# Attention and two gated feed-forward layers: the issue order of all engines is chosen by a search over priorities

## The chip, the core and the metric

The kernel runs on one core of a Trainium2 chip. The core has five engines that run their own instruction queues in order: TensorE (PE, matrix products, with its weight loads shown apart as PEld), VectorE (DVE), ScalarE (ACT), GpSimd (POOL) and SyncE (SP, which issues the DMA transfers here). An instruction waits until the semaphores it names have been raised, and all that stands behind it on its engine waits with it. The metric is the device time of one execution in microseconds (us).

## The reference

Two batches of eight heads, 768 positions, head size 64. Each position attends to the 31 positions around it and to 24 block summaries (maximum of the keys, mean of the values, over blocks of 32). The result, 1536 tokens of 512, goes through two feed-forward layers.

```python
k_sum = k.reshape(B, H, nb, block, D).max(axis=3)
v_sum = v.reshape(B, H, nb, block, D).mean(axis=3)
scores_l = scale * np.matmul(q, k.transpose(0, 1, 3, 2))      # kept where |i - j| < 16
scores_s = scale * np.einsum('bhsd,bhnd->bhsn', q, k_sum) + np.log(block)
a = softmax(concatenate([scores_l, scores_s]))
x = a @ concatenate([v, v_sum])                # -> 1536 x 512
x = (silu(x @ w_gate) * (x @ w_val)) @ w_out   # d_ff 1536
h = x @ w_in2
out = (h * tanh(softplus(h))) @ w_out2         # d_ff 2048
```

## The kernel before

**Attention** is cut into 24 units: batch, third of the sequence, pair of heads (four pairs). A unit has a piece on TensorE for the scores (`scores`, S below, line 468), on VectorE four passes that add the mask and take the extreme (line 504), on ScalarE four exponentials (line 521), on VectorE the division (lines 534 to 544), on TensorE four transposes (`transposes`, T, line 558) whose result ScalarE copies out of PSUM, and on TensorE the products with the values (`values`, V, line 573). ScalarE and VectorE then cut the result into two fp32r halves `xh` and `xl`. Units 0 to 3 are those of the first 256 tokens.

**The means** of the values of batch 0 (`means_first`) are six products of line 346 (M below), one for each of six loads m0 to m5, added up in PSUM bank 0. Four copies then bring the result into `vext`, the value windows: pair 0 and 2 on ScalarE (line 279), 1 and 3 on VectorE (line 285). All four read bank 0. Every V of the first batch needs its pair's copy.

**Weights** come as 64-bit words of a float64 array in loads of 512 KB (`words32`, t0, t1, ... below, into three buffers `raw`); ScalarE (line 725) and VectorE (lines 732, 741, 752) make 32-bit floats of them, and the two engines cut these into fp32r halves in `wsl`. The first three are the gate, value and output weights of chunk 0.

**The feed-forward work** is a list of items (chunk of the hidden size, token group). The first items have 256 tokens. H below is a product of line 822 (hidden layer), O one of lines 873 and 921 (output layer). Later units of seven block products use line 1179. At the end of a run of items VectorE adds the output banks to `pacc` (line 952), and a new run may write the bank only after that.

**The order.** The kernel does not issue as it goes. `Program.add` records operations with an engine, a cost, the keys they read and write, and at times a wanted time. `Program.order` then goes through them with a list scheduler on a model: each engine takes the ready operation with the earliest latest time. What it gives is the order in which every engine's queue is written. The model sees handover times, DMA times and costs as constants; nothing of it exists on the chip. The loads of the beginning have wanted times from `FIRST_LOADS`: k, q are the keys and queries of a unit, c0 and c1 the two halves of the constants (masks; last mask, identity and mean matrix), m the mean loads, w the value windows of a unit, t the weights.

**Fills.** Where the model sees TensorE idle before line 873 begins, `order` puts products on a constant tile (`warm`, line 266, W below). They compute nothing that is used.

**Loads** share eight semaphores in turn, so that a load is issued only when the eighth before it has landed.

Of the kernel before, what the change touches and what calls it, by code (L numbers as in the profile page):

```python
# [56 lines left out]

JOIN, PAIRED = 6, 12


FIRST_LOADS = "k0 q0 k1 c0 q1 k2 c1 q2 k3 q3 t0 t1 m0 m1 m2 m3 m4 m5 w0 w1 w2 w3 t2".split()
# [36 lines left out]
class Program:  # L98
# [3 lines left out]
    def __init__(self):  # L102
        self.ops = []

        self.fill, self.fill_to = None, 0
        self.last_write = {}
        self.readers = {}

    def add(self, eng, cost, fn, r=(), w=(), want=None, rel=0.0):
# [15 lines left out]
        self.ops.append(dict(eng=eng, cost=cost, fn=fn, deps=sorted(deps), want=want, rel=rel))  # L125

    def order(self):
# [6 lines left out]
        dma_latency, hop = 3200.0, 250.0  # L134
        own = dict(PE=0.0, ACT=120.0, DVE=120.0, POOL=120.0, SP=0.0)
        late = [0.0] * len(ops)
        for n in range(len(ops) - 1, -1, -1):
            o = ops[n]
            t = min((late[s] for s in after[n]), default=1e9) - o["cost"] - hop
            if o["eng"] == "SP":  # L140
                t -= dma_latency
            late[n] = t if o["want"] is None else min(t, o["want"])
        left = [len(o["deps"]) for o in ops]
        ready = [o["rel"] for o in ops]
        free = dict.fromkeys(own, 0.0)
        dma_free = 1000.0
        waiting = {e: [n for n, o in enumerate(ops) if o["eng"] == e and not left[n]] for e in own}
        done = []
        while any(waiting.values()):
            best = None  # L150
            for e, c in waiting.items():
                if c:
                    t = max(free[e], min(ready[n] for n in c))
                    if e == "SP":
                        t = max(t, dma_free - 1500.0)
                    if best is None or t < best[0]:
                        best = (t, e)
# [4 lines left out]
            if e == "PE" and self.fill:  # L162
                gap = t - free["PE"]
                done += [self.fill] * (FILL_FIRST if not free["PE"] else max(0, int(FILL * gap / 430.0)))
                if n == self.fill_to:
                    self.fill = None
            done.append(o["fn"])
            if e == "SP":
                free[e] = t + 450.0
                dma_free = max(dma_free, t) + o["cost"]  # L170
                end = dma_free + dma_latency
            else:
                free[e] = end = t + o["cost"]
            for s in after[n]:
# [4 lines left out]
        return done  # L179
# [10 lines left out]
def c_pool(n):  # L190
    return 100 + 2.35 * n
# [7 lines left out]
def tile_kernel(  # L199
# [47 lines left out]
    vrows = vx[:, 0 : NPAIR * 512].rearrange("k (n c) -> k n c", c=DM)  # L247
    vext = [vrows[:, :, p * P : (p + 1) * P] for p in range(NPAIR)]
# [27 lines left out]
    def copy(dst, src, n, psum, r, w, scale=1.0, eng="ACT"):  # L276
# [3 lines left out]
        elif eng == "POOL":  # L280
            assert scale == 1.0
            cost, fn = c_pool(n) * 1.5, lambda: nc.gpsimd.tensor_copy(out=dst, in_=src)
# [85 lines left out]
    def means_second(side):  # L368
# [22 lines left out]
        op("PE", 920, products, r=[*used, "cst1"], w=[("bank", bk)])  # L391
# [84 lines left out]
    def scores(*of):  # L476
        vals = held.pop(of[0], [])
        made = [score_products(i) for i in of]
        cost = 530 * len(vals) + 410 * len(of) + 250 + 130 * (len(vals) > 0) + (300 if of[0] < NPAIR else 0)
# [13 lines left out]
    def softmax(i):  # L493
# [46 lines left out]
        op("DVE", 100, lambda: nc.vector.reciprocal(out=t[:, 2, :], in_=t[:, 2, :]), w=[kt_])  # L540
# [22 lines left out]
    def values(i):  # L563
# [29 lines left out]
        op("PE", 640, products, r=r, w=w, want=wanted_at(i) + 9e3)  # L593
# [27 lines left out]
    for step in steps:  # L621
        stage[step[0]](int(step[1:]))
# [84 lines left out]
    def words32(name, c):  # L707

        k = counts["raw"]
        counts["raw"] += 1  # L710
        rw, a, q = raw[k % NRAW], cva[k % NCV], cvs[k % NCV]
        kr, ka, kq = ("raw", k % NRAW), ("cva", k % NCV), ("cvs", k % NCV)
        src = w_src[name][c].bitcast(U32)
        if len(src.shape) == 3:
# [9 lines left out]
            650,  # L724
# [22 lines left out]
        if name in "gvo":  # L747
            return f32(a), ka
# [8 lines left out]
        )  # L757
        return f32(a), ka
# [484 lines left out]
    for n, it in enumerate(items):  # L1243
        if it[0] == 1 and it[4] == GRP:
            clock["rate"] = 1.0
        (block_item if it in blocked else silu_item)(n)
        while prev <= n - lag[n]:
            out_products(prev)
            prev += 1
        if n == first_s - AHEAD:  # L1250
# [61 lines left out]
```

## Time and profile before

| what | value |
|---|---|
| three timed runs | 605.57, 606.43, 609.68 us, median 606.43 us |
| the profiled execution's own time | 605.46 us |
| its span, first to last instruction | 603.5 us |
| TensorE busy | 594.7 us, 99% |
| VectorE, ScalarE, GpSimd busy | 443.8 us (74%), 332.3 us (55%), 25.0 us (4%) |
| granted TensorE clock, mean | 0.999 |

TensorE's busy time holds the fills and matmuls that are drawn out by waits in their pipeline, so it is to be read stage by stage and against the pace of the same products elsewhere. The chain that ended last is TensorE for 93% of the span.

### The profile page before, as it was taken

The page shows a single profiled execution, that of the slowest core. Times are in us where ns is not written, and L with a number is a line of the kernel's source. Part 1 is how long each engine was busy: PE and PEld are TensorE (multiplying, and loading weights), DVE is VectorE, ACT ScalarE, POOL GpSimd, SP SyncE. Part 2 cuts the span into 40 slices and gives each one's busy share as a digit, 9 for nine tenths or more (in the row PEclk, how much of TensorE's full clock was granted, in tenths as well). Part 3 has the DMA queues.
Part 4 walks back from the last instruction along what each step waited for, and adds up shares of the span by engine and source line. Part 5 has one row for each costly group of instructions (what it writes and reads, how often), then busy time and mean ns, then how long its engine had stood idle before and what let it go on. Part 6 is the DMA issues. An engine that isn't in the chain of part 4 may idle for free.

```text
span 603.5 us, 10209 instructions
## 1 busy us (share of the span) xinstructions
PE 594.7 (99%) x3858; PEld 507.2 (84%) x3858; DVE 443.8 (74%) x1005; ACT 332.3 (55%) x764; POOL 25.0 (4%) x37
## 2 busy tenths in 40 slices
PE   8999999999999999999999999999999999999997
PEld 6688899988988889988889778988888889988875
DVE  6898689687498958858948999996574476972333
ACT  4787689655464635634525666766553465643230
POOL 3213220000000000000000000000000000000000
PEclk9999999999999999999999999999999999999999
DMA  9988566004100321302401301332130040300103
GB/s 321 303 240 220 128 197 201 29 6 153 52 1 0 141 70 45 133 33 71 141 0 33 108 2 35 105 140 84 56 107 34 1 139 1 106 0 1 70 1 139
DMA packets 34768, 55.02 MB, mean 91 GB/s; under 512 B 8712, under 2 KB 23176, under 8 KB 34720
## 3 DMA queue, kind: packets, MB, share of 16 engines
q1 hardware_dynamic: 34720, 54.38, 28.4%
q8 instruction: 30, 0.49, 0.3%
q14 instruction: 18, 0.15, 0.1%
HBM read 50.98 MB, written 3.15 MB: 90 GB/s over the span
## 4 chain that ended last, share of the span: by engine, by line
PE 93%; DVE 3%; DMA 2%; ACT 1%; issue 0%; SPq 0%; DVEq 0%
PE bank L1179 38%; PE bank L921 34%; PE bank L822 11%; PE bank L873 3%; PE bank L468 2%; PE bank L573 2%; PE bank L558 2%; DMA raw<-in_w_gate_dram 1%; DVE pacc L952 1%; PE bank L346 1%; DMA att<-in_qt_dram 1%; DVE pacc L293 1%; PE bank L266 0%; DVE xl L1079 0%; PE bank L382 0%
## 5 line engine op out<-in xcount | busy, mean ns | idle before, releaser
L1179 PE MATMUL bank<-xh,wsl 128*128 128x256 f32 (+1 forms) x512 | 142.5, 336 | 0.0
L921 PE MATMUL bank<-wsl,gt 128*128 128x512 f32 x576 | 139.1, 390 | 0.2 <-DVE pacc L952 0.2
L921 PEld LDWEIGHTS bank<-wsl,gt 128*128 128x128 f32 x576 | 106.0, 188 | 20.8 <-ACT gt L279 0.6
L1179 PEld LDWEIGHTS bank<-xh,wsl 128*128 128x128 f32 x512 | 92.0, 189 | 11.2
L293 DVE TENSOR_TENSOR tmps<-tmps,bank 128x256 f32<-128x256 f32 (+1 forms) x93 | 51.3, 551 | 66.9 <-PE bank L1179 56.5
L921 PE MATMUL bank<-gt,wsl 128*128 128x512 f32 x360 | 92.3, 392 | 1.0 <-DVE pacc L952 0.6
L1179 PE MATMUL bank<-att_late,wsl 128*128 128x512 f32 (+1 forms) x352 | 86.8, 370 | 0.0
L1179 PE MATMUL bank<-xl,wsl 128*128 128x256 f32 (+1 forms) x256 | 85.9, 336 | 0.0
L279 ACT ACTIVATE wsl<-cva 128x512 fp32r<-128x512 f32 (+1 forms) x100 | 59.1, 594 | 41.7 <-DVE cva L752 10.1
L921 PEld LDWEIGHTS bank<-gt,wsl 128*128 128x128 f32 x360 | 65.7, 188 | 14.9 <-DVE pacc L952 2.0
L822 PE MATMUL bank<-xh,wsl 128*128 128x256 f32 (+1 forms) x288 | 77.9, 328 | 0.3 <-DVE tmps L1131 0.3
L1179 PEld LDWEIGHTS bank<-att_late,wsl 128*128 128x128 f32 x352 | 64.8, 188 | 12.1 <-ACT tmps L279 0.2
L293 DVE TENSOR_TENSOR wsl<-cva,wsl 128x512 fp32r<-128x512 f32 (+1 forms) x100 | 63.8, 644 | 11.4 <-ACT wsl L279 9.9
L279 ACT ACTIVATE tmps<-bank 128x512 f32<-128x512 f32 (+1 forms) x80 | 39.1, 491 | 56.4 <-PE bank L1179 49.8
L293 DVE TENSOR_TENSOR gt<-tmps,gt 128x512 fp32r<-128x512 f32 (+1 forms) x77 | 49.6, 644 | 25.7 <-PE bank L921 13.9
L279 ACT ACTIVATE gt<-tmps 128x512 fp32r<-128x512 f32 (+1 forms) x76 | 44.9, 591 | 29.7 <-PE bank L921 21.8
L1201 ACT ACTIVATE tmps<-tmps 128x512 f32<-128x512 f32 (+1 forms) x66 | 34.5, 522 | 48.3 <-DVE tmps L293 48.1
L822 PEld LDWEIGHTS bank<-xh,wsl 128*128 128x128 f32 x288 | 51.6, 189 | 6.8 <-issue 1.8
L1179 PEld LDWEIGHTS bank<-xl,wsl 128*128 128x128 f32 x256 | 48.4, 189 | 6.3
L741 DVE SCALAR_TENSOR_TENSOR cva<-cvs,cva 128x512 uint32<-128x512 uint32 x68 | 46.7, 691 | 1.2
L725 ACT ACTIVATE cvs<-raw 128x512 f32<-128x512 f32 x68 | 45.0, 667 | 3.5 <-DMA raw<-in_w_val_dram 1.7
L822 PE MATMUL bank<-xl,wsl 128*128 128x256 f32 (+1 forms) x144 | 45.8, 318 | 0.0
(104 smaller groups left out, 721.1 us busy)
## 6 DMA issues: line engine op xcount, KB each, us to landing
raw<-in_w_out_dram SPq DMA_DIRECT2D x28, 512.0 KB, 3.7
raw<-in_w_in_dram SPq DMA_DIRECT2D x16, 512.0 KB, 3.6
raw<-in_w_gate_dram SPq DMA_DIRECT2D x12, 512.0 KB, 3.5
raw<-in_w_val_dram SPq DMA_DIRECT2D x12, 512.0 KB
att<-in_vt_dram SPq DMA_DIRECT2D x24, 192.0 KB, 5.4
att<-in_qt_dram SPq DMA_DIRECT2D x24, 128.0 KB, 4.5
out_dram<-pacc SPq DMA_DIRECT2D x8, 256.0 KB, 2.1
pacc<-in_kt_dram SPq DMA_DIRECT2D x4, 400.0 KB, 5.0
```

The source lines that it names most:

```text
L279: cost, fn = c_act(n, psum), lambda: nc.scalar.activation(out=dst, in_=src, func=AF.Copy, scale=scale)
L293: op(eng, c_dve(n), lambda: nc.vector.tensor_tensor(out=dst, in0=a, in1=b, op=alu), r=r, w=w)
L468: nc.tensor.matmul(parts_[2 * j + n // 2][q, cols], qb[d, n, :], moving, start=True, stop=True)
L558: nc.tensor.transpose(ps[0:KC, n * P : (n + 1) * P], s[:, n * KC : (n + 1) * KC], ident)
L573: nc.tensor.matmul(ps[d, n * TQ : (n + 1) * TQ], ve[:, n, d], pt[:, at : at + TQ], start=True, stop=True)
L725: lambda: nc.scalar.activation(out=f32(q), in_=f32(high), scale=2.0**-112, **signed),
L741: lambda: nc.vector.scalar_tensor_tensor(out=a, in0=q, scalar=3, in1=a, op0=ALU.logical_shift_left, op1=ALU.bitwise_or),
L822: nc.tensor.matmul(ps, a, x, start=(kk == 0 and m == 0), stop=(kk == KD - 1 and m == 2))
L873: nc.tensor.matmul(bank[bk][:, col : col + HALF], w[:, a, mm], gg[:, x, 0:sz], start=(n in starts and both == 1 and q == 0 and m % 2 == 0) ...
L921: nc.tensor.matmul(bank[m], lhs, rhs, start=(n in starts and both == 1 and q == 0), stop=(n in ends and both == 0),)
L1179: nc.tensor.matmul(banks[b][:, 0:wide], w, v()[:, kk, :], start=(start and kk == 0 and m == 0), stop=(kk == 1 and m == 2), skip_group_chec ...
L1201: op("ACT", c_act(wide), lambda: nc.scalar.activation(out=y, in_=src, func=func), r=r, w=[*k, *free])
```

## The change

`order` now calls the list scheduler (moved into `issued`) 601 times: first as it is, then with shifts of the priorities of groups of operations, drawn with a fixed seed, of which each is kept if the model's last TensorE operation does not end later. Only groups with a latest time under 110 us are shifted. The model itself has other constants: handover 170 ns instead of 250, starting times for the engines, a DMA that lands 1650 ns after its bytes and at most eight loads in flight, VectorE and GpSimd not at once on what the model takes for a shared port, and other costs for some TensorE pieces, GpSimd copies and one ScalarE conversion. `FIRST_LOADS` has c0, c1 and the mean loads further ahead. The four value windows `vext` lie one behind the other in `att` instead of interleaved by 128 columns. The arithmetic is the same; the number of fills is what the new order makes it.

```diff
-FIRST_LOADS = "k0 q0 k1 c0 q1 k2 c1 q2 k3 q3 t0 t1 m0 m1 m2 m3 m4 m5 w0 w1 w2 w3 t2".split()
+RECIP = 100
+SEARCH, SEARCHED = 600, 110e3
+FIRST_LOADS = "k0 q0 c0 k1 q1 c1 m0 m1 k2 q2 k3 q3 m2 m3 t0 m4 m5 t1 w0 w1 w2 w3 t2".split()
...
+        groups = sorted({o["group"] for n, o in enumerate(ops) if o["group"] and late[n] < SEARCHED})
+        rng, shift = random.Random(0), dict.fromkeys(groups, 0.0)
+
+        def issue(shift):
+            return self.issued(after, [t + shift.get(o["group"], 0.0) for t, o in zip(late, ops)])
+
+        best, issued = issue(shift)
+        for _ in range(SEARCH):
+            other = dict(shift)
+            for g in rng.choices(groups, k=rng.choice((1, 1, 2, 4))):
+                other[g] += rng.gauss(0.0, 4e3)
+            end, seq = issue(other)
+            if end <= best:
+                best, issued, shift = end, seq, other
...
-        dma_latency, hop = 3200.0, 250.0
-        own = dict(PE=0.0, ACT=120.0, DVE=120.0, POOL=120.0, SP=0.0)
+        hop = 170.0
+        own = dict(PE=0.0, ACT=100.0, DVE=60.0, POOL=60.0, SP=0.0)
...
                     if e == "SP":
-                        t = max(t, dma_free - 1500.0)
+                        t = max(t, landed[-8] + 150.0)
...
-                dma_free = max(dma_free, t) + o["cost"]
-                end = dma_free + dma_latency
+                dma_free = max(dma_free, t + 900.0) + o["cost"] * 1.08
+                end = dma_free + 1650.0
+                landed.append(end)
             else:
+                if o["port"]:
+                    t = max(t, port["DVE" if e == "POOL" else "POOL"])
+                    port[e] = t + o["cost"]
...
-def c_pool(n):
-    return 100 + 2.35 * n
+def c_pool(n, runs=True):
+    return 170 + (0.85 if runs else 2.1) * n
...
-    vrows = vx[:, 0 : NPAIR * 512].rearrange("k (n c) -> k n c", c=DM)
-    vext = [vrows[:, :, p * P : (p + 1) * P] for p in range(NPAIR)]
+    vext = [vx[:, p * 512 : (p + 1) * 512].rearrange("k (n c) -> k n c", c=P) for p in range(NPAIR)]
...
-        op("PE", 920, products, r=[*used, "cst1"], w=[("bank", bk)])
+        op("PE", 1180, products, r=[*used, "cst1"], w=[("bank", bk)])
...
-        op("PE", 640, products, r=r, w=w, want=wanted_at(i) + 9e3)
+        op("PE", 800, products, r=r, w=w, want=wanted_at(i) + 9e3)
```

**The loads, SyncE, from the fifth issue on.** `pacc` takes the keys (k2 and k3 in `pacc1`), `att` the queries and, 96 partitions high, the value windows, `cst` the constants, `raw` weights, `tmps` and `att_tmp` the mean loads. Before:

```order
L274 DMA att_90<-in_qt_dram 128x256
L274 DMA pacc1_88<-in_kt_dram 128x800
L274 DMA cst_69<-in_consts_dram 128x388
L274 DMA att_90<-in_qt_dram 128x256
L274 DMA pacc1_88<-in_kt_dram 128x800
L274 DMA att_90<-in_qt_dram 128x256
L274 DMA raw0_77<-in_w_gate_dram 128x1024
L274 DMA raw1_78<-in_w_val_dram 128x1024
L274 DMA tmps_92<-in_vt_dram 128x512 x3
L274 DMA att_tmp_91<-in_vt_dram 128x512
L274 DMA tmps_92<-in_vt_dram 128x512 x2
L274 DMA att_90<-in_vt_dram 96x4x128 x4
```

Of the change, from the seventh issue on:

```order
L312 DMA pacc1_88<-in_kt_dram 128x800
L312 DMA tmps_92<-in_vt_dram 128x512
L312 DMA att_90<-in_qt_dram 128x256
L312 DMA tmps_92<-in_vt_dram 128x512
L312 DMA pacc1_88<-in_kt_dram 128x800
L312 DMA raw0_77<-in_w_gate_dram 128x1024
L312 DMA att_90<-in_qt_dram 128x256
L312 DMA tmps_92<-in_vt_dram 128x512
L312 DMA att_tmp_91<-in_vt_dram 128x512
L312 DMA tmps_92<-in_vt_dram 128x512
L312 DMA raw1_78<-in_w_val_dram 128x1024
L312 DMA tmps_92<-in_vt_dram 128x512
```

The mean loads stand between k2 and the fourth query load now, and t1 (`raw1`) has gone from the twelfth to the seventeenth place; the four windows are the nineteenth to twenty-second load in both.

**TensorE around the transposes of unit 4.** `bank3` takes the transposes, `bank2` the values, banks 4 and 5 hidden products; `warm` is a fill. Before:

```order
L822 MATMUL bank5_66<-xh0_70,wsl_76 128x256
L822 MATMUL bank5_66<-xl0_73,wsl_76 128x256
L822 MATMUL bank5_66<-xh0_70,wsl_76 128x256
L558 MATMUL bank3_64<-cst_69,att_tmp_91 120x128 x4
L266 MATMUL bank1_62<-warm_98 128x256 x3
L573 MATMUL bank2_63<-att_tmp_91,att_90 64x64 x8
```

Of the change:

```order
L597 MATMUL bank3_64<-cst_69,att_tmp_91 120x128 x4
L865 MATMUL bank5_66<-xh0_70,wsl_76 128x256
L865 MATMUL bank5_66<-xl0_73,wsl_76 128x256
L865 MATMUL bank5_66<-xh0_70,wsl_76 128x256 x2
L865 MATMUL bank5_66<-xl0_73,wsl_76 128x256
L865 MATMUL bank5_66<-xh0_70,wsl_76 128x256 x2
L865 MATMUL bank5_66<-xl0_73,wsl_76 128x256
L865 MATMUL bank5_66<-xh0_70,wsl_76 128x256
L612 MATMUL bank2_63<-att_tmp_91,att_90 64x64 x8
```

Nine hidden products stand between the transposes and the values of unit 4 in place of three fills.

**VectorE at the last run of the first layer.** `pacc` with a bank is an addition of line 952 (995 in the change), `pacc` alone and `xl` prepare the second layer's input. Before:

```order
L952 TENSOR_TENSOR pacc1_88<-pacc1_88,bank3_64 128x512
L293 TENSOR_TENSOR gt1_85<-tmps_92,gt1_85 128x512
L1079 TENSOR_TENSOR xl0_73<-pacc0_87,xh0_70 128x1024
L293 TENSOR_TENSOR wsl_76<-cva1_81,wsl_76 128x256
L293 TENSOR_TENSOR pacc0_87<-pacc1_88,pacc0_87 128x1024
L1079 TENSOR_TENSOR xl1_74<-pacc1_88,xh1_71 128x1024
L293 TENSOR_TENSOR pacc1_88<-pacc1_88 128x1024
L952 TENSOR_TENSOR pacc0_87<-pacc0_87,bank2_63 128x512
L293 TENSOR_TENSOR pacc1_88<-pacc1_88,pacc0_87 128x1024
L952 TENSOR_TENSOR pacc0_87<-pacc0_87,bank3_64 128x512
```

Of the change:

```order
L995 TENSOR_TENSOR pacc1_88<-pacc1_88,bank3_64 128x512
L331 TENSOR_TENSOR gt1_85<-tmps_92,gt1_85 128x512
L1122 TENSOR_TENSOR xl0_73<-pacc0_87,xh0_70 128x1024
L1122 TENSOR_TENSOR xl1_74<-pacc1_88,xh1_71 128x1024
L331 TENSOR_TENSOR pacc0_87<-pacc1_88,pacc0_87 128x1024
L995 TENSOR_TENSOR pacc0_87<-pacc0_87,bank2_63 128x512
L331 TENSOR_TENSOR pacc1_88<-pacc1_88 128x1024
L995 TENSOR_TENSOR pacc0_87<-pacc0_87,bank3_64 128x512
```

The addition from `bank2` has one operation of 1024 columns and the `wsl` operation less ahead of it.

## Rows read from the trace of the kernel before

**Rows 1.** The page: busy us of each engine (share of the span, instructions).
```profile
PE 594.7 (99%) x3858; PEld 507.2 (84%) x3858; DVE 443.8 (74%) x1005; ACT 332.3 (55%) x764; POOL 25.0 (4%) x37
```

**Rows 2.** Windows: stretch, length, busy per engine PE to POOL, clock, DMA share, GB/s.
```profile
0.00:24.45 24.45, 21.60 (x242) 14.97 (x242) 16.81 (x59) 14.13 (x46) 6.51 (x12) 1.00 0.98 318
24.45:39.90 15.45, 15.14 (x177) 12.82 (x173) 14.92 (x52) 12.61 (x41) 5.34 (x7) 1.00 1.06 299
39.90:117.00 77.10, 76.90 (x1015) 70.20 (x1011) 63.18 (x266) 59.93 (x217) 13.17 (x18) 1.00 0.57 160
117.00:338.00 221.00, 221.00 (x1142) 189.53 (x1139) 172.82 (x324) 109.85 (x206) 0.00 (x0) 1.00 0.19 66
338.00:352.00 14.00, 13.04 (x54) 9.52 (x53) 13.93 (x19) 9.67 (x13) 0.00 (x0) 1.00 0.07 28
```

**Rows 3.** Timeline of SyncE: start, length, issue, count.
```profile
9.88 0.80 SPq L274 DMA_DIRECT2D tmps<-in_vt_dram  x2
...
18.60 0.33 SPq L274 DMA_DIRECT2D att<-in_qt_dram  x1
...
22.13 1.98 SPq L274 DMA_DIRECT2D att<-in_vt_dram  x3
```

**Rows 4.** Chain that ended last, first 60 us: start, length, what.
```profile
17.84 2.59 PE bank L346 x6
...
20.45 0.60 ACT att L279
...
21.08 0.71 DVE att L285
...
26.30 7.18 DMA raw<-in_w_gate_dram
```

**Rows 5.** Timeline of TensorE, 24 to 40 us (idle before, and its releaser).
```profile
24.45 0.39 PE L822 MATMUL bank<-xh,wsl 128*128 128x256 f32 x1
...
25.27 1.02 PE L266 MATMUL bank<-warm 128*128 128x256 f32 x4
25.94 0.47 PE L822 MATMUL bank<-xh,wsl 128*128 128x256 f32 x1
...
27.61 1.46 PE L266 MATMUL bank<-warm 128*128 128x256 f32 x6
29.00 0.64 PE L468 MATMUL bank<-kx,att 64*64 64x120 f32 x16
...
32.97 1.46 PE L266 MATMUL bank<-warm 128*128 128x256 f32 x6
...
35.93 0.39 PE L822 MATMUL bank<-xh,wsl 128*128 128x256 f32 x1 [0.31 <-DVE tmps L1131]
...
39.90 0.38 PE L822 MATMUL bank<-xh,wsl 128*128 128x256 f32 x1
```

**Rows 6.** Timeline of TensorE at 97 us: output products, then hidden products.
```profile
97.15 0.40 PE L873 MATMUL bank<-gt,wsl 128*128 128x256 f32 x2
97.39 0.28 PE L822 MATMUL bank<-xh,wsl 128*128 128x256 f32 x1
```

**Rows 7.** Timeline of TensorE, 338 to 352 us.
```profile
346.32 1.98 PE L921 MATMUL bank<-gt,wsl 128*128 128x512 f32 x8
348.62 1.43 PE L921 MATMUL bank<-gt,wsl 128*128 128x512 f32 x5 [0.33 <-DVE pacc L952]
350.36 1.42 PE L921 MATMUL bank<-gt,wsl 128*128 128x512 f32 x5 [0.30 <-DVE pacc L952]
351.62 0.39 PE L1179 MATMUL bank<-xh,wsl 128*128 128x512 f32 x1
```

**Rows 8.** Chain that ended last, from 346 us: start, length, what.
```profile
346.84 1.14 DVE pacc L293
347.97 0.60 DVE pacc L952
...
413.86 9.55 PE bank L921 x42
```

More of the change, by code (lines that the diff above doesn't have):

```diff
@@ L103, in __init__ @@
         self.ops = []
-        self.fill, self.fill_to = None, 0
+        self.fill, self.fill_to, self.group = None, 0, None
         self.last_write = {}
@@ L124, in add @@
         deps.discard(n)
-        self.ops.append(dict(eng=eng, cost=cost, fn=fn, deps=sorted(deps), want=want, rel=rel))
+        free = cost == RECIP or any(key[0] in ("bank", "ksm") for key in (*r, *w))
+        port = eng == "POOL" or (eng == "DVE" and not free)
+        self.ops.append(dict(eng=eng, cost=cost, fn=fn, deps=sorted(deps), want=want, rel=rel, port=port, group=self.group))
     def order(self):
@@ L161, in order @@
             o = ops[n]
[L162 to L167, printed above, removed]
             if e == "SP":
                 free[e] = t + 450.0
-                dma_free = max(dma_free, t) + o["cost"]
-                end = dma_free + dma_latency
-            else:
+                dma_free = max(dma_free, t + 900.0) + o["cost"] * 1.08
+                end = dma_free + 1650.0
+                landed.append(end)
+            else:
+                if o["port"]:
+                    t = max(t, port["DVE" if e == "POOL" else "POOL"])
+                    port[e] = t + o["cost"]
                 free[e] = end = t + o["cost"]
+                if e == "PE":
+                    pe_end = end
+            seq.append((e, t, end, n))
             for s in after[n]:
@@ L281, in copy @@
             assert scale == 1.0
[L282 removed]
+            cost, fn = c_pool(n, n != HALF), lambda: nc.gpsimd.tensor_copy(out=dst, in_=src)
         else:
@@ L539, in softmax @@
         )
-        op("DVE", 100, lambda: nc.vector.reciprocal(out=t[:, 2, :], in_=t[:, 2, :]), w=[kt_])
+        op("DVE", RECIP, lambda: nc.vector.reciprocal(out=t[:, 2, :], in_=t[:, 2, :]), w=[kt_])
         op(
@@ L621, in tile_kernel @@
     for step in steps:
+        pg.group = ("unit", int(step[1:]))
         stage[step[0]](int(step[1:]))
@@ L710, in words32 @@
         counts["raw"] += 1
+        was, pg.group = pg.group, ("words", k)
         rw, a, q = raw[k % NRAW], cva[k % NCV], cvs[k % NCV]
@@ L747, in words32 @@
         if name in "gvo":
+            pg.group = was
             return f32(a), ka
@@ L757, in words32 @@
         )
+        pg.group = was
         return f32(a), ka
@@ L1245, in tile_kernel @@
             clock["rate"] = 1.0
+        pg.group = ("item", n)
         (block_item if it in blocked else silu_item)(n)
         while prev <= n - lag[n]:
+            pg.group = ("out", prev)
             out_products(prev)
             prev += 1
+        pg.group = ("blocks", n)
         if n == first_s - AHEAD:
```

32 lines of the change are left out of this document (24 added, 8 removed).

## The prediction

> **What bounds the kernel now.** I read the page first, then the busy time by stretches, then the chain and the timeline where a stretch is not full. The page says that TensorE is busy for 594.7 of 603.5 us [rows 1], and from 117 to 338 us it is busy for all 221.00 us [rows 2]. An order cannot make the products there fewer, so nothing is to be had in that stretch. The places that an order can reach are the beginning, to 24.45 us, when the first hidden product starts; the stretch to 39.90 us, in which 8 fills stand; the mixed stretch to 117 us; and 338 to 352 us, where TensorE shows 13.04 of 14.00 us while VectorE is full with 13.93 [rows 2]. In the first 40 us the DMA engines are saturated too (shares 0.98 and 1.06), so loads can change places there, but the bytes do not come faster.
>
> **A, the beginning: the mean loads go between the key loads.** Before, TensorE makes the six means after all scores, in two pieces of three, and ends the second, 2.59 us long, at 20.43 [rows 4]; so one mean costs 0.86 us. In the change four of them stand earlier, in the gaps between scores and transposes. What then ends the means is the last load, m5. It is the eighteenth load in both orders. Before, the twenty-sixth issue, which waits for the eighteenth landing, goes at 18.60 [rows 3]; the bytes ahead of m5 are the same loads in both, so I leave it there. Then the last mean ends at 18.6 + 0.86 = about 19.5, and the four copies begin some 0.8 us sooner than at 20.45.
>
> The four copies alternate between ScalarE and VectorE, 0.60 and 0.71 us, each starting where the other ends [rows 4]: 2.6 us for the four. All four read bank 0, in the change as before; only their destinations have moved apart. I take them to alternate still; side by side on the two engines they would take 1.3 us less.
>
> The Trainium skill, PSUM — Partial Sum Buffer, section "PSUM bank collisions raise a hardware error", says that two engines must not be in the same bank and quadrant at once, two reads included, whatever the addresses. By that the new layout brings the copies nothing; without it they could overlap. The alternation in the rows agrees with the page, and no run here shows them side by side.
>
> So the fourth copy ends at about 22.2 instead of 23.1. Little of that arrives: the windows w0 to w3 are the nineteenth to twenty-second loads as before, and the thirtieth issue shows the last of them landed at 22.13 [rows 3]; and ScalarE now has the upper half of t1's weights between the means and the copies of unit 1's and unit 3's transposes (0.6 us, as a copy of 512 columns takes in [rows 4]), which the last two V wait for. I put the first hidden product at 24.25 instead of 24.45: **-0.2 us**. Bounds: -1.3 (the copies side by side) and +0.9 (one more mean of 0.86 on the path, since the scores of units 2 and 3 stand behind m0 and m1 now, and wait where these land late).
>
> **B, 24.45 to 39.90: fills and one stall.** Two fills run for 25.94 - 25.27 = 0.67 us, three for 29.00 - 27.61 = 1.39, and three more from 32.97 on, whose row is as long as that of the three before [rows 5]: 3.45 us for 8, 0.43 each. The change has 5 in this stretch, 2.15 us. That saves 1.3 us if what stands behind is ready. At the largest place it is: after unit 4's transposes nine hidden products at 0.12 us (two products of the same length take 97.39 - 97.15 = 0.24 [rows 6]) make 1.08 us and cover ScalarE's copy of 0.6. Further, TensorE idles 0.31 us at 35.93 for VectorE, line 1131 [rows 5]; that VectorE operation stands behind the conversion of a gate weight whose load took 7.18 us from 26.30 to 33.48 [rows 4], on which it blocks in order. In the change that load is issued after two query loads and one window, but ahead of an output weight of 512 KB that stood ahead of it, and VectorE takes the conversion only after the divisions and the line that TensorE needs. **-1.6 us** (1.3 + 0.3). Bounds: 0, each dropped fill turned into a wait, and -3.8, all fills and the idle time gone. I stay nearest the counted fills.
>
> **C, 39.90 to 117: fewer changes of kind.** From the last fill to the last unit TensorE changes 144 times between kinds of work before, 112 times after; those between hidden and output products go from 62 to 29, the others from 82 to 83. A change between these two costs nothing: two output products take 0.24 us to the next start [rows 6]. Only the first product behind an attention piece is longer, 0.38 against 0.28 us ([rows 5], at 39.90, and [rows 6]). So **0**, with -3.3 (33 at 0.1 us) as the other bound; I take the end whose row is the same pair of kinds. VectorE at 63.18 and ScalarE at 59.93 of 77.10 us [rows 2] leave room to follow.
>
> **D, 338 to 352: the additions.** Undisturbed, 42 products of this form take 9.55 us, 0.227 each [rows 8]. From 346.32 to 348.62 eight take 2.30 instead of 1.82 us, then five 1.74 and five 1.26 instead of 1.14 [rows 7]: 0.48, 0.60 and 0.12, together 1.2 us, in which TensorE waits for additions (line 952) to empty its banks. The addition that ends the first begins at 347.97, directly behind 1.14 us of `pacc` work [rows 8], which the change puts behind it; a `wsl` operation has gone from ahead of it too. It starts at least 1.14 us sooner then, more than the first stall, and the second addition moves with it. TensorE's stalls end; the idle time at 341 us for ScalarE stays. **-1.1 us**; bounds 0 (the whole chain of VectorE starts as much later) and -1.6 (the idle time goes too).
>
> **The rest costs nothing.** The model's constants, the port rule and the costs exist only while the order is made. The window loads have runs of 128 columns on the side they are read from in both layouts, so their transfers do not get larger. The eight semaphores that the loads share were there before. Between 117 and 338 us pieces change places, but TensorE is full before and the products are the same.
>
> **Sum.** -0.2 - 1.6 - 1.1 = -2.9 us on the profiled execution's 605.46 gives 602.6 us. The median of the three timed runs lies 0.97 above that execution, the lowest 0.11; by the median the sum is 603.5. I forecast the middle, **603.0 us**, 0.6% below the median.
>
> **Rivals.**
> *Given back.* TensorE arrives 2 us sooner at work that VectorE and ScalarE must have ready; they are 82% and 78% busy to 117 us and VectorE 97% to 39.90 [rows 2], in an order that the model only thinks fits. For it: VectorE is full in 24 to 40 us, so a head start there can only come out of its 0.5 us of idle time or of work put off. Against it: TensorE shows only 0.20 us of idle time in 77.10 there, so the inputs now come early. Then the time is that of D alone or of nothing, 605.0.
> *All bounds together.* A -0.9, B -2.6 (three quarters of the fills' time), C -1.5, D -1.6: -6.6, 599.3. For it: the order was searched over the whole beginning, not for the fills alone. Against it: the VectorE share just named.
> *Slower.* t1 goes from the twelfth to the seventeenth place, and its conversion stands on ScalarE ahead of the first copy of the means and on VectorE ahead of the second. The seventeenth issue was at 9.88 [rows 3]; with the 7.18 us that a weight load took [rows 4] t1 lands at 17.1, and the copies need it by about 18.9 (two conversions before 20.3, of about 0.7 us each like the copies of 512 columns in the same group). Each us beyond that holds both engines, and with them every V and the first product, for one us. From 21.8 on the whole gain is gone, and landing at 24 gives 2.2 us more than before, 608. Against it: 1.8 us of room.
> *The order does not do what it says* is the first of these: the fills go and waits stand in their place.
>
> **Chances.** Forecast (600.5 to 604.5) 0.65; given back 0.20; all bounds 0.10; slower 0.05. One per cent, about what a measurement of this kernel can tell from no change, is 6.1 us; only the third reaches below 600.4, and not always: faster 0.09. Above 612.5 only a multiple of the fourth: slower 0.03. Within: 0.88. The range for 8 in 10 runs from 599.9 to 605.9: it takes in the given-back case and most of the third.
>
> **What would show it.** Right: the first hidden product at about 24.3 us; five fills after it; the hidden product that stands at 39.90 now (first of the second 256 tokens) at about 38.1; no idle time of TensorE for line 995 in the last run of the first layer; the stretch that follows as full as before. Wrong: idle time before V or S in place of the fills, which gives B back; two of the mean copies at the same time, which makes A -1.3; the first product after 24.6, which points to t1 or m1; or new idle time in 40 to 117 us, which is the first rival.

## The result, and the profile after

| | before | after |
|---|---|---|
| median, range | 606.69 us, 605.57 to 609.68 (6 runs) | 611.92 us, 610.88 to 612.72 (6 runs) |
| profiled execution, span | 605.46 us, 603.5 us | 612.72 us, 610.7 us |

Here the kernel before has three more runs than ahead of the prediction. The change makes the kernel 0.8% slower: ratio 1.008, interval 1.0056 to 1.0104. The prediction was 603.0 us, 599.9 to 605.9.

The page of after, the line of [rows 1]:

```profile
PE 599.9 (98%) x3854; PEld 505.4 (83%) x3854; DVE 446.1 (73%) x1005; ACT 334.1 (55%) x764; POOL 24.2 (4%) x37
```

The windows of after, the stretches of [rows 2] and the one behind them (length, busy time of PE to POOL, clock, DMA share, GB/s):

```profile
0.00:24.45 24.45, 21.93 (x228) 15.02 (x228) 16.71 (x57) 13.70 (x45) 6.82 (x13) 1.00 0.97 312
24.45:39.90 15.45, 15.37 (x191) 13.36 (x189) 14.77 (x55) 13.15 (x44) 5.17 (x7) 1.00 0.95 269
39.90:117.00 77.10, 76.23 (x979) 69.26 (x979) 63.63 (x263) 59.29 (x214) 12.26 (x18) 1.00 0.57 168
117.00:338.00 221.00, 219.71 (x1150) 185.68 (x1149) 171.09 (x322) 109.95 (x208) 0.00 (x0) 1.00 0.19 63
338.00:352.00 14.00, 13.73 (x60) 10.70 (x59) 14.00 (x21) 7.95 (x12) 0.00 (x0) 1.00 0.20 75
352.00:380.00 28.00, 26.71 (x117) 21.15 (x116) 26.83 (x41) 19.15 (x30) 0.00 (x0) 1.00 0.06 20
```

and the last of these stretches in the kernel before:

```profile
352.00:380.00 28.00, 28.00 (x139) 23.58 (x138) 28.00 (x46) 18.47 (x33) 0.00 (x0) 1.00 0.12 36
```

TensorE is no longer busy for all of 117 to 338 us, and the busy time of its weight loads fell from 189.53 [rows 2] to 185.68 us there. Busy time hides much of what is lost, since a drawn-out product counts as busy. So I take from the timeline the start of every product, subtract the pace of its kind (0.227 us for 512 columns [rows 8], 0.12 for 256 [rows 6], the median of its own kind for the small ones), and call what is left, fills included, **lost**:

| stretch, us | step of the prediction | lost before | lost after | difference |
|---|---|---|---|---|
| 0 to 41 | A, B | 18.5 | 17.9 | -0.6 |
| 41 to 117 | C | 7.0 | 7.4 | +0.4 |
| 117 to 130 | the rest | 0.2 | 2.0 | +1.8 |
| 130 to 338 | the rest | 0.5 | 2.6 | +2.1 |
| 338 to 352 | D | 2.1 | 0.8 | -1.2 |
| 352 to 380 | behind D | 0.1 | 2.2 | +2.1 |
| 380 to the end | the rest | 5.3 | 7.9 | +2.6 |

Together 7.2 us, the difference of the two spans. The level of the first two rows hangs on the pace that is taken for the small products; the differences between kernels there hold to about 0.5 us (0.8 in `hop250` below). Of the last row, 4.6 us in both kernels lie behind the start of the last product. The stretches to 117 us and the additions (D) gain 1.4 us net; stretches that were full lose 8.6. Three things make that up.

**Many short breaks.** Waits of TensorE's weight loads from 117 us to the end (in total, times, longest), before:

```profile
PEld bank L1179 <- ACT tmps L279: 0.2, 1, 0.2
```

and after:

```profile
PEld bank L1222 <- ACT tmps L317: 7.5, 24, 1.3
PEld bank L1222 <- ACT kx L317: 1.0, 4, 0.3
```

A block product (line 1179 before, 1222 after) writes a bank that ScalarE first has to copy out (`keep`). One such place in the timeline of after:

```profile
222.28 0.41 PEld L1222 LDWEIGHTS bank<-att_late,wsl 128*128 128x128 f32 x2
222.73 0.87 PEld L964 LDWEIGHTS bank<-gt,wsl 128*128 128x128 f32 x4
222.96 1.07 PE L964 MATMUL bank<-gt,wsl 128*128 128x512 f32 x4
223.22 0.60 ACT L317 ACTIVATE tmps<-bank 128x512 f32<-128x512 f32 x1
223.87 1.23 PEld L1222 LDWEIGHTS bank<-att_late,wsl 128*128 128x128 f32 x6 [0.27 <-ACT tmps L317]
223.87 1.66 PE L1222 MATMUL bank<-att_late,wsl 128*128 128x512 f32 x6
```

and six such products without a break, the same view at 367 us:

```profile
367.05 1.52 PE L1222 MATMUL bank<-att_late,wsl 128*128 128x512 f32 x6
```

As a rule a weight load lies under the product before it: the one at 222.73 starts 0.23 us ahead of its product at 222.96. At 223.87 load and product start together, and the six take 1.66 instead of 1.52 us. The model is not wrong about the time: it puts the copy at 0.479 us, adds the new handover of 0.170 and has the bank free 0.65 us after 223.22, at 223.87, which is when the load went. It does not know that TensorE must have the bank before that if nothing is to be lost. In 130 to 338 and 380 to 590 us there are 31 places after, and 3 before, at which a product loses over 0.06 us. They lose 3.4 us together, against 0.5 before; the rest of the 4.7 us that these two stretches lose more is in smaller pieces. With handovers of 250 ns (`switch` and `hop250` below) such places are all but gone.

The Trainium skill, TensorE: Matmul & The Clock Gate, section "Architectural detail: the array is 16× 32×32, not 1× 128×128", says that TensorE's queue can pull weight loads ahead of matmuls in flight. The loads that lie under the product before (222.73 under 222.96) agree. A held load costs about 0.11 us here.

**A function table load without cover.** Timeline of ScalarE and of TensorE after, at 126 us:

```profile
125.97 1.28 ACT L1166 ACT_TABLE_LOAD   x1 [1.92 <-PE bank L865]
127.26 0.60 ACT L1166 ACTIVATE tmps<-bank 128x512 f32<-128x512 f32 x1
```
```profile
129.77 1.42 PE L964 MATMUL bank<-gt,wsl 128*128 128x512 f32 x5 [1.17 <-ACT gt L317]
```

The first silu of 512 columns loads another table. In the kernel before it did so at 120.30 us, with other work for TensorE still at hand; after, the load starts when the gate product ends, and TensorE runs out of work.

**The border of the two layers.** In the kernel before VectorE is full from 352 to 380 us (28.00 of 28.00), so what it loses there TensorE loses too. After D, a second table load (first mish) at 362.80 holds ScalarE; VectorE waits 1.17 us for a conversion that stands behind it, ScalarE then for VectorE, TensorE for ScalarE. Rows of ScalarE, VectorE, ScalarE and TensorE after:

```profile
362.80 1.28 ACT L1244 ACT_TABLE_LOAD   x1
```
```profile
366.46 0.69 DVE L331 TENSOR_TENSOR wsl<-cva,wsl 128x512 fp32r<-128x512 f32 x1 [1.17 <-ACT wsl L317]
```
```profile
369.60 0.63 ACT L1118 ACTIVATE xh<-kx 128x512 fp32r<-128x512 f32 x1 [1.64 <-DVE kx L331]
```
```profile
370.76 1.43 PE L1222 MATMUL bank<-att_late,wsl 128*128 128x512 f32 x5 [0.83 <-ACT tmps L317]
```

### The profile page after: what moved, and what is told of

Its sections match the earlier page's. It is cut to its first block, busy times and chain, and to the rows that moved or that the text cites. A ratio compares the mean times of both kernels' runs of the same rounds, so it can differ in the third digit from the quotient of the medians.

```text
span 610.7 us, 10192 instructions
## 1 busy us (share of the span) xinstructions
PE 599.9 (98%) x3854; PEld 505.4 (83%) x3854; DVE 446.1 (73%) x1005; ACT 334.1 (55%) x764; POOL 24.2 (4%) x37
## 4 chain that ended last, share of the span: by engine, by line
PE 74%; DVE 17%; ACT 3%; DMA 2%; issue 2%; SPq 1%; DVEq 0%; ACTq 0%
PE bank L1222 31%; PE bank L964 28%; PE bank L865 9%; DMA tmps<-in_vt_dram 2%; PE bank L916 2%; DVE cva L782 2%; DVE wsl L331 2%; DVE gt L331 2%; PE bank L612 1%; DVE pacc L995 1%; DVE tmps L331 1%; DVE cva L773 1%; DVE xl L1122 1%; PE bank L506 1%; PE bank L597 1%
## 5 line engine op out<-in xcount | busy, mean ns | idle before, releaser
L1222 PE MATMUL bank<-xh,wsl 128*128 128x256 f32 (+1 forms) x512 | 142.7, 337 | 0.1
L964 PE MATMUL bank<-wsl,gt 128*128 128x512 f32 x576 | 137.0, 390 | 0.2 <-DVE pacc L995 0.2
L1222 PEld LDWEIGHTS bank<-xh,wsl 128*128 128x128 f32 x512 | 91.8, 189 | 12.1 <-DVE kx L331 1.0
L964 PE MATMUL bank<-gt,wsl 128*128 128x512 f32 x360 | 90.7, 392 | 1.9 <-ACT gt L317 1.2
L1222 PE MATMUL bank<-att_late,wsl 128*128 128x512 f32 (+1 forms) x352 | 89.1, 376 | 1.0 <-ACT tmps L317 0.8
L865 PE MATMUL bank<-xh,wsl 128*128 128x256 f32 (+1 forms) x288 | 74.1, 327 | 0.0
L865 PEld LDWEIGHTS bank<-xh,wsl 128*128 128x128 f32 x288 | 50.1, 189 | 5.4 <-issue 0.9
```

The source lines that it names most:

```text
L865: nc.tensor.matmul(ps, a, x, start=(kk == 0 and m == 0), stop=(kk == KD - 1 and m == 2))
L964: nc.tensor.matmul(bank[m], lhs, rhs, start=(n in starts and both == 1 and q == 0), stop=(n in ends and both == 0),)
L1222: nc.tensor.matmul(banks[b][:, 0:wide], w, v()[:, kk, :], start=(start and kk == 0 and m == 0), stop=(kk == 1 and m == 2), skip_group_chec ...
```

## The experiments

In all of them the arithmetic is the same. The edits are shown in their main lines. The table gives the time lost by stretch in each one's profiled execution, as above, the places over 0.06 us ("breaks"), and the ratio to the kernel before.

| kernel | 0-41 | 41-117 | 117-130 | 130-338 | 338-380 | 380-end | breaks | ratio (interval) |
|---|---|---|---|---|---|---|---|---|
| before | 18.5 | 7.0 | 0.2 | 0.5 | 2.2 | 5.3 | 3 | 1 |
| after | 17.9 | 7.4 | 2.0 | 2.6 | 3.0 | 7.9 | 31 | 1.008 (1.0056 to 1.0104) |
| switch | 19.6 | 7.7 | 0.6 | 1.5 | 5.3 | 5.3 | 3 | 1.0046 (1.0031 to 1.0061) |
| before170 | 18.2 | 9.1 | 0.3 | 2.3 | 3.0 | 7.1 | 23 | 1.008 (1.0061 to 1.0099) |
| nosearch | 18.9 | 9.9 | 0.3 | 2.5 | 3.0 | 7.6 | 28 | 1.0114 (1.0096 to 1.0132) |
| hop250 | 23.1 | 6.0 | 0.7 | 0.6 | 5.3 | 5.3 | 1 | 1.0092 (1.0071 to 1.0113) |
| old566 | 17.9 | 6.7 | 0.0 | 0.5 | 5.3 | 5.3 | 2 | 1.0038 (1.0025 to 1.0051) |
| old255 | 19.6 | 6.9 | 0.3 | 0.5 | 3.9 | 5.3 | 1 | 1.0031 (1.0018 to 1.0044) |
| pairs | 19.9 | 6.4 | 0.5 | 0.5 | 1.9 | 5.4 | 2 | 1.0002 (0.9993 to 1.0012) |
| measured | 19.8 | 6.5 | 0.4 | 0.7 | 1.7 | 5.3 | 2 | 0.9988 (0.9977 to 0.9999) |
| loads_alone | 19.6 | 7.6 | 0.4 | 0.7 | 2.1 | 5.3 | 3 | 1.0012 (1.0001 to 1.0024) |
| table170 | 20.0 | 7.2 | 0.1 | 2.6 | 2.0 | 7.8 | 28 | 1.01 (1.0076 to 1.0124) |
| measured_old | 19.2 | 6.3 | 0.7 | 0.6 | 1.5 | 5.9 | 4 | 0.9979 (0.9967 to 0.9992) |
| late_search | 19.3 | 6.3 | 0.1 | 0.6 | 1.4 | 5.5 | 3 | 0.9989 (0.9979 to 0.9998) |

### Which part costs: the handover or the search

Handover of before from 117 us on (`switch`), handover of the change alone (`before170`), the change without its search (`nosearch`), the change with the handover of before throughout (`hop250`):

```diff
 switch, in issued(), last pass only
+            if t > until:   # 117e3
+                hop, own = 250.0, dict(PE=0.0, ACT=120.0, DVE=120.0, POOL=120.0, SP=0.0)
 before170, in order() of before
-        dma_latency, hop = 3200.0, 250.0
+        dma_latency, hop = 3200.0, 170.0   # own: ACT 100, DVE and POOL 60
 nosearch
-SEARCH, SEARCHED = 600, 110e3
+SEARCH, SEARCHED = 0, 110e3
 hop250, in issued()
-        hop = 170.0
+        hop = 250.0                        # own: 120
```

> The change with one difference: the search runs as it is, but the order that is issued goes over to the old handover times (250 ns to another engine, 120 to the own) where the model's clock passes 117 us; up to there every queue is the change's. In the change TensorE loses as much as before up to 120 us (25.4 us against 25.6), and 7 us more behind it: 1.7 in 120 to 130 us, where it waits 1.2 us for the first gt of 512 columns, some 2 in 130 to 338 and 3 from 380 on in breaks of 0.1 us before block products, 1.6 in 352 to 380. Theory 'handover': the shorter handover lets the model put TensorE, ScalarE and VectorE at their inputs as these come ready, and on the chip they come later; this kernel then gets back 5 to 7 us: 604.5 to 607 us. Rival 'search': the shifted priorities leave a worse state behind at 117 us; then this kernel keeps the loss: 610 to 613. Rival 'table': the two long waits come from the two function table loads on ScalarE of 1.28 us, which fall where they fall; then only the short breaks go: 607 to 609.

> The kernel before with the new handover times alone (170 ns to another engine, 100 on ScalarE, 60 on VectorE and GpSimd, in place of 250 and 120) in the pass that issues; priorities, costs, loads and layout are those of before. 'Handover': it loses most of what the change loses, 610 to 613 us, with breaks of 0.1 us before block products by the dozen. 'Search': as before, 605.5 to 607.5. 'Table': the short breaks alone, 608 to 610.

> The change without the search (0 tries in place of 600); model, loads and layout are the change's. 'Handover': as slow as the change, 610 to 614 us. 'Search': as before or better, 604 to 607.5. 'Table': the short breaks stay, the long waits may move: 608 to 612.

> The change with the old handover times (250 and 120 ns) in the model throughout, so that the search works on them too; everything else is the change's. 'Handover': 603 to 607 us, few breaks before block products. 'Search': 610 or more. 'Table': 607 to 609.

Measured: 610.28, 611.84, 614.08 and 612.77 us. The search is not what costs: without it the change is slower still (18.9 + 9.9 us lost up to 117 us instead of 17.9 + 7.4). The handover alone, put into the kernel before, costs as much as the whole change, 23 breaks among it:

```profile
PEld bank L1179 <- ACT tmps L279: 7.3, 25, 1.2
```

and with 250 ns behind 117 us the breaks are gone (3 and 1). But `switch` and `hop250` did not come down to 607: at the border they lose 5.3 us, more than before and after. `hop250` also loses 23.1 us in the beginning, where the granted clock was 0.79 on average in 25 to 41 us; `switch`, whose queues are the change's up to 117 us, lost 1.7 us more than it there, since a query load landed later in that execution and the clock was 0.79 on average in 8 to 16 us. Their times lie in the range of the rival 'search', which `nosearch` speaks against. So 'handover' was right on the breaks and wrong as the whole story; 'table' fits `switch` no better, whose loss at 128 us became one of 0.74 at 132. The beginning is not the same in two executions of the same queues either, as `switch` and the change show, so a difference of some 2 us there says little about an order.

### Is the border a matter of the draw

What `switch` and `hop250` share at the border with each other but not with the kernel before is, among other constants, the price of ScalarE's conversion. `old566` is before with that price, `old255` is before with a handover longer by 5 ns:

```diff
 old566
-            650,
+            566,
 old255, in the pass that issues
-        dma_latency, hop = 3200.0, 250.0
+        dma_latency, hop = 3200.0, 255.0
```

> The kernel before with one number of its model changed: ScalarE's conversion of a weight half costs 566 in place of 650 ns, as in the change. Everything else is that of before, the handover of 250 ns too. In 338 to 380 us TensorE loses 2.2 us in the kernel before, 3.0 in the change, in the change without search and in the kernel before with the short handover, and 5.3 in the two kernels that had the long handover and 566. Theory 'draw' (how VectorE's full queue at the border of the two layers comes to stand is settled by small numbers, and before has a good case): 5.3 us lost there, few breaks elsewhere, 609 to 611 us. Rival 'handover alone': a conversion's price is of no account, 606 to 608.

> The kernel before with a handover of 255 ns in the model's pass in place of 250; all other numbers are its own. Some 100 of TensorE's 2180 rows stand elsewhere. Theory 'draw': five ns mean nothing on the chip, but another order comes of them, and before's border of the layers is a good case: 3 to 5 us lost in 338 to 380 in place of 2.2, 608 to 611 us. Rival 'handover alone': as before, 606 to 608.

Measured: 608.81 and 608.37 us, 0.38% and 0.31% over before, with 5.3 and 3.9 us lost at the border and hardly a break. `old566` is a little faster than was expected, 'draw' holds for both. Neither number was chosen for the border. A model that differs by 5 ns in one constant writes another order, and at the border, where VectorE has almost no idle time (13.93 of 14.00 us in [rows 2], 14.00 after), TensorE loses between 1.4 and 5.3 us over all the kernels of the table. The kernel before, with 2.2, has a good case of it. So part of every comparison of two orders here is that draw: 3.1 and 1.7 us at the border in these two.

### The handover by pair of engines, and the table loads

`pairs` is the change with the handovers that the traces show and a margin for TensorE's weight load; `measured` also knows the table loads, and searches further; `table170` is the change with the table loads alone:

```diff
 pairs
-        hop = 170.0
-        own = dict(PE=0.0, ACT=100.0, DVE=60.0, POOL=60.0, SP=0.0)
+        own = dict(PE=0.0, ACT=105.0, DVE=100.0, POOL=60.0, SP=0.0)
+        hop = {(a, b): 330.0 if b == "PE" else 200.0 if a == "PE" else 143.0 for a in own for b in own}
+        hop |= {(e, e): own[e] for e in own} | {("SP", e): 170.0 for e in own if e != "SP"}
 measured: that, and (table170: this alone)
+                if o["table"] and o["table"] not in tables:
+                    tables.add(o["table"])
+                    t += 1283.0
 measured
-SEARCH, SEARCHED = 600, 110e3
+SEARCH, SEARCHED = 3300, 400e3
```

> The change with handovers in the model by the pair of engines, from the traces: 330 ns to TensorE (170 to its weight load, 108 by which a product is longer when that load has nothing to hide behind, and some 50 of margin), 200 from TensorE (a 512-column product takes 0.427 us from its start to ScalarE's start, at a pace of 0.227), 143 between ScalarE and VectorE, 105 and 100 on the own engine; the search works on these. Theory 'handover': the breaks of 0.1 us before block products go (31 in the change, 3 or fewer here), which gives back about 3 us; the two long waits by ScalarE's function table loads can stay, since the model does not know these: 604 to 609 us. Rival 'draw': the breaks go, but the border of the layers takes it back: 609 to 612.

> As the kernel with handovers by pair, and the model also holds ScalarE for 1.283 us at the first silu of 512 columns and at the first mish (the two function table loads in the traces, at 126.0 and 362.8 us in the change); the search goes over groups due up to 400 us with 3300 tries, so that the border of the layers is in it. Theory 'the model lacked what the chip charges': no wait over 0.5 us behind 117 us but at the border, less than 2 us lost in 338 to 380, hardly a break: faster than before, 602 to 605.5 us. Rival 'draw': what the model finds does not hold on the chip, 606 to 611.

> The change with one thing added to its model: ScalarE is held for 1.283 us at the first silu of 512 columns and at the first mish, as in the traces (table loads). The handover stays at 170 ns. Theory: the 1.3 us that TensorE waits at 128 us goes, the wait of 1.0 us at 370 goes or shrinks, and the breaks of 0.1 us stay (25 to 35 of them): 608.5 to 610.5 us, two of the five us. Rival, that the long waits come from the short handover like the breaks: they stay, 611 to 613.

Measured: 606.40, 605.78 and 612.92 us. `pairs` is the change in all but these numbers, and it is as fast as before: with these handovers, all of the 5.2 us come back. No weight load of a block product waits for ScalarE's `keep` copies there any more, and the border loses 1.9 us. In `table170` the waits at 128 and 370 us are gone (117 to 130: 0.1 instead of 2.0; 352 to 380: 1.2 instead of 2.2) and the breaks are not (28 remain). That fits the rows above, in which the waits follow the table loads. For 128 us it is no proof: `before170` and `nosearch`, whose models do not know the table loads, lose only 0.3 us there, with another order. At 370 to 372 us both still wait, by 0.81 and 0.83 us. `table170` missed the time that was expected of it, since its beginning lost 2.1 us more than the change's, and in three of its six runs the mean granted clock was 0.993 and the time 613.9 to 614.5, against 610.9 to 612.0 in the others. `measured` lost 1.7 us at the border, as expected, but its beginning 19.8; its 605.78 us lie between the ranges of theory and rival, 0.1% below before.

### The beginning

`loads_alone` is before with the new `FIRST_LOADS` line, `measured_old` is `measured` with the old one, `late_search` is that with no group searched that holds anything due in the first 20 us:

```diff
 late_search
-        groups = sorted({... if o["group"] and late[n] < SEARCHED})
+        groups = sorted({... if o["group"] and late[n] < SEARCHED} - {o["group"] for n, o in enumerate(ops) if late[n] < 20e3})
```

> The kernel before with the change's FIRST_LOADS alone (constants and mean loads further ahead); model and layout are those of before. In the trace of the change the last mean load was issued at 10.17 and landed at 19.35 us, the last mean ended at 20.5 as in the kernel before (20.43), and the first hidden product stood at 25.27 us against 24.45. Theory 'late m5' (the move of the mean loads does not bring the last one, on which all four copies wait): means end at 20.3 to 20.6, first hidden product not before 24.4, 605.5 to 608 us. Rival 'step A as it was forecast': means end at about 19.5, first hidden product at about 24.25, 0.2 us and what follows from it less than before, 605 to 606.5.

> The kernel with handovers by pair and table loads in its model (3300 tries, groups due up to 400 us), with the FIRST_LOADS of the kernel before. That kernel lost 26.3 us up to 117 us, the kernel before 25.5, the change 25.3. If the new order of loads is what costs the beginning there: 25 to 25.8 us lost up to 117 and 604 to 605.5 us. If the search's order costs it: as with the new loads, 605 to 606.5.

> As the kernel with handovers by pair, table loads in the model and the loads of before, with the search kept from all groups that hold anything due before 20 us, so that the loads and pieces of the beginning stand in the plain order; groups due from there to 400 us are searched. In the kernel ahead of it the search issued a weight load first of all, TensorE then stood idle for 3.2 us from 4.5 us on, and the granted clock was 0.50 from 8 to 14 us. Theory 'what is left is the beginning's clock and the border': no stretch under full clock, 25 to 26 us lost up to 117 us (before: 25.5), under 2 lost in 338 to 380 (2.2), hardly a break: 604 to 605.5 us in every run, with less spread. Rival 'the searched beginning was worth more than its clock cost': 605.5 to 607.

Measured: 607.39, 605.41 and 605.75 us. In `loads_alone` the means ended at 18.5 us, sooner than both theories said, and the first hidden product still stood at 24.66. Its chain of what ended last:

```profile
10.83 8.44 DMA raw<-in_w_val_dram
19.27 0.02 issue
19.29 0.69 ACT cvs L725
19.98 0.02 issue
20.00 0.60 ACT att L279
```

That is the mechanism of the prediction's rival 'slower': t1's conversion stands on ScalarE ahead of the copies, and t1 landed at 19.27. `measured_old` and `late_search` come out below before by 0.2% and 0.1%, as `measured` does by 0.1%; the intervals end just short of 1 and overlap each other. `measured_old` lost 25.5 us up to 117 us, as it was expected if the new order of loads is what costs, but its 605.41 us fit both of its cases. The median of `late_search`, 605.75, lies in the range of its rival. In the profiled execution of `measured_old` the clock is low: its search put a weight load first, TensorE stood idle from 4.52 to 7.74 us, and the windows show (PEclk third from the end):

```profile
4.00:6.00 2.00, 0.52 (x3) 0.11 (x1) 1.36 (x3) 0.88 (x2) 0.58 (x1) 1.00 0.98 336
6.00:8.00 2.00, 0.26 (x8) 0.29 (x8) 2.00 (x3) 0.43 (x1) 2.00 (x3) 0.86 1.03 376
8.00:10.00 2.00, 1.80 (x48) 1.50 (x48) 1.57 (x7) 0.16 (x1) 2.00 (x3) 0.50 1.06 388
...
12.00:14.00 2.00, 2.00 (x16) 1.17 (x19) 2.00 (x5) 0.98 (x6) 0.86 (x2) 0.50 1.04 397
14.00:16.00 2.00, 2.00 (x38) 1.20 (x36) 1.05 (x3) 0.67 (x1) 0.00 (x0) 0.93 1.06 408
```

Five of its twelve runs have a mean clock of 0.993 or 0.994 and take 605.6 to 606.7 us, the other seven 0.997 to 1.0 and 604.2 to 606.8. `late_search` keeps the full clock in the beginning, with the smallest span of all, 603.0 us.

## Why the prediction was wrong

**The step that failed is "The rest costs nothing".** It took "the model's constants ... exist only while the order is made" as a reason for a price of nothing, and the argument that from 117 to 338 us TensorE "is full before and the products are the same". The products are the same, but full was a property of the old order, not of the stretch. An order cannot make it shorter, and it can make it longer: 1.8 + 2.1 + 2.6 us there, and 2.1 behind D. The diff had it in plain sight (handover 170 instead of 250); what it asks is which margin TensorE's inputs had. `before170` shows that the shorter handover alone brings 23 of the 31 breaks and costs 0.8%; `switch`, `hop250` and `pairs`, with longer ones, have 1 to 3 breaks, and `pairs` is as fast as before. Open is how much of the time is the draw: `hop250` has one break and is still 0.9% slower, with 4.6 us more lost in the beginning than before and 3.1 more at the border, so some of what `pairs` regains may be a good order there. The other constants, the port rule and the layout of `vext` were not tried alone; `pairs` holds them all.

**A was wrong by its size, +0.75 for -0.2** (25.20 against 24.45 us), near its upper bound of +0.9. The term that was mis-sized is the landing of m5, which was put at 18.6. The chain of after:

```profile
5.09 5.06 DMA tmps<-in_vt_dram
...
10.17 9.18 DMA tmps<-in_vt_dram
...
19.39 1.13 PE bank L384 x2
...
20.55 0.60 ACT att L317
```

m5 landed at 19.35, the last mean took 1.13 us for 0.86; the means ended where they ended before (20.43 [rows 4]), and the copies began at 20.55 instead of the forecast's 19.5. In the change m5 is issued behind the 512 KB of t1 (and only m0 and m1 stand ahead of the fourth query load, not all mean loads):

```profile
9.53 0.44 SPq L312 DMA_DIRECT2D raw<-in_w_val_dram  x1
10.17 0.33 SPq L312 DMA_DIRECT2D tmps<-in_vt_dram  x1
```

In `loads_alone` m5 is issued ahead of t1, at 10.46 us against 10.83, and the wait of the last mean's weight load for it ends 2 us sooner than in the change. After, then `loads_alone`:

```profile
19.39 0.28 PEld L384 LDWEIGHTS bank<-tmps,cst 128*120 128x120 f32 x2 [1.45 <-DMA tmps<-in_vt_dram]
```
```profile
17.39 0.28 PEld L346 LDWEIGHTS bank<-tmps,cst 128*120 128x120 f32 x2 [0.83 <-DMA tmps<-in_vt_dram]
```

So with DMA engines full (0.97 of the stretch), the one of these two that is issued last lands at 19.3 us, m5 in the change, t1 (19.27) in `loads_alone`. t1 was said to land at 17.1 from an undisturbed load's 7.18 us; in the change VectorE waits for it until 18.39, still ahead of the 18.9 at which the copies need it. The other terms of A held. The copies alternate as in [rows 4], and the upper half of t1's weights (`wsl`) takes 0.6 us of ScalarE between them and the `att_tmp` copies:

```profile
20.55 0.59 ACT L317 ACTIVATE att<-bank 24x512 f32<-24x512 f32 x1 [1.08 <-PE bank L384]
21.17 0.70 DVE L323 COPY att<-bank 24x512 f32<-24x512 f32 x1 [0.77 <-ACT att L317]
21.90 0.59 ACT L317 ACTIVATE att<-bank 24x512 f32<-24x512 f32 x1 [0.76 <-DVE att L323]
22.52 0.63 ACT L317 ACTIVATE wsl<-cva 128x512 fp32r<-128x512 f32 x1
...
23.93 0.60 ACT L317 ACTIVATE att_tmp<-bank 120x512 f32<-120x512 f32 x1
```

The last of these rows in the kernel before:

```profile
23.18 0.60 ACT L279 ACTIVATE att_tmp<-bank 120x512 f32<-120x512 f32 x1
```

That is the whole 0.75 us: 0.10 from copies that begin at 20.55 instead of 20.45, the rest from `wsl`. Each copy is released by the one before it, which is what the program orders; no run shows what the bank itself would do.

**B was right in mechanism: -1.3 for -1.6.** Five fills stand between the first hidden product and the forty-ninth, in place of eight, and that product, at 39.90 in [rows 5], is at

```profile
39.37 0.39 PE L865 MATMUL bank<-xh,wsl 128*128 128x256 f32 x1
```

so that the stretch is 39.37 - 25.20 = 14.17 us in place of 15.45. The fills take 2.17 instead of 3.45 us and the wait at 35.93 is gone, both as forecast; two more output products stand in the stretch, 0.26 us that the forecast did not count. (The forty-ninth is the first of the second 256 tokens in the change; in the kernel before it still belongs to the first 256, which the prediction had wrong.)

**C was right: +0.4 for 0.** Fewer changes of kind brought nothing that shows. The idle time grew from 0.20 us to 0.87 (76.23 busy of 77.10), and most of the 0.6 us that were gained before 41 us was given back, the first rival.

**D was right, also in mechanism: -1.2 for -1.1.** The addition now begins 0.32 us after the products that wait for it (350.41 and 350.09 below), in place of 1.65 (347.97 [rows 8] and 346.32 [rows 7]), and these run without a break. One wait for line 995 is left in the stretch, 0.27 us, at the place of the wait for ScalarE that was to stay:

```profile
350.41 0.60 DVE pacc L995
```
```profile
350.09 2.20 PE L964 MATMUL bank<-gt,wsl 128*128 128x512 f32 x9
```
```profile
345.23 3.66 PE L964 MATMUL bank<-gt,wsl 128*128 128x512 f32 x14 [0.27 <-DVE pacc L995]
```

But "the whole chain of VectorE starts as much later" was only asked within 14 us. In 352 to 380 us it all came back and more (2.1 us).

**The rivals.** 'Slower' had the nearest number, 608, but by a mechanism that was not at work in the change, where t1 came in time for the copies. It was at work in `loads_alone`, where the first hidden product came 0.21 us later than before. 'Given back' had the mechanism of the beginning and the wrong place for the loss. None of them looked at the full stretches behind 117 us.

## What to carry to other kernels

When a change touches the numbers of a scheduler's model, every stretch that its order fills is part of the change: ask first for the stretches that are full now, because there it can only lose. The time at which an input is ready is not the time at which TensorE wants it: here a weight load that did not go under the product before cost 0.11 us. So a handover to TensorE needs a margin over what the trace shows from end to start. And before a gain of half a per cent is credited to a search, move one constant of the model by a few ns and measure that: here 5 ns moved the time by 0.3%.

## What the runs showed of the hardware that was not expected

- A weight load that a wait holds until its product's turn costs TensorE about 0.11 us, though no idle time shows before the product (six products 1.66 instead of 1.52 us at 223.87, of which the first is the drawn-out one).
- A function table load takes 1.28 us on ScalarE, and the function starts right behind it (125.97 + 1.28, then 127.26). The Trainium skill, ScalarE: Activation LUTs, section "What ACT_TABLE_LOAD costs", gives 1283 ns, which agrees, and a drain of some 1380 ns with it; behind the load the rows leave no room for one, 0.01 us to the silu.
- In the profiled execution of `measured_old`, after 3.2 us without a product, the granted clock was 0.50, the 1.2 GHz level, from 8 to 14 us, and 0.93 in 14 to 16; the search's model has no clock. The ratio of that kernel is still the lowest.
- In the beginning a load of 256 KB issued at 10.17 us, just behind one of 512 KB, took 9.18 us to land; in `loads_alone` the same load, issued at 10.46 just ahead of the 512 KB, had landed by 17.39, and the 512 KB took 8.44 us from 10.83. Here the place in the queue counted, not the size.
